# Thirteen transfers instead of sixteen for out = x + alpha·fx, with two operands sharing one buffer

## The chip, the cores and the metric

The kernel runs on one core of one Trainium2 chip, alone. The metric is the device time of the program in microseconds (us). It is a median over runs of the same program, and the profile comes from one further, profiled execution.

## The reference

```
B, S, D = 512, 32, 640          # x, fx: bfloat16, alpha: one bfloat16
def reference(x, fx, alpha):
    return x + alpha * fx
```

The arrays x and fx hold 512 · 32 · 640 values of two bytes each, 20.97 MB each, and the output is as large. So 62.9 MB cross between memory and the core's on-chip buffer whatever the kernel does, and the arithmetic is one multiply and one add for each value.

## The kernel before

Every array is seen as 128 partitions of 81,920 values. A partition's stretch is counted in columns of 512 values (K = 512), which are 1 KiB in bfloat16. There are N = 160 columns, so x alone takes 160 KiB of each partition. x has a place for the whole of itself in the buffer (`xt`), and the sum is written over it. fx has a pool `fs` of two buffers of 23 columns each (46 KiB), through which its pieces pass in turn. Together that is 206 columns.

Three lists cut the work. `X` has the six pieces in which x is loaded, `F` the seven pieces of fx, and `S` the three pieces in which the result is stored. Each piece is one transfer of all 128 partitions, so a piece of c columns is 128 rows of c KiB.

The order is written out by hand in `PLAN`, one step to a line: `x i` and `f j` load a piece, `c j` computes, `s i` stores, and `a` loads alpha and spreads it over the partitions (a matmul with a row of ones, then a copy, lines 111 to 115). All transfers are issued by SyncE (line 78), and its queue works strictly in the order of the plan: a transfer that has to wait holds up every one that stands behind it. All of `c` is VectorE's. For a piece of fx it first multiplies fx by alpha in place (line 96), then adds it onto x in place (line 99).

What makes a transfer wait in the kernel before is the pool. The third piece of fx goes into the buffer of the first, so `f 2` stands after `c 0` and waits for it, and so on for each later piece. x has no such waits, because every column of it has a place of its own. The first store is additionally held until the last piece of fx has landed (`LATE`). The last six columns of x (`x 5`) stand between that piece and the stores. The steps that the change and the prediction speak of are `load_x`, `load_f`, `compute` and `store`, with the lists above.

Of the kernel before, what the change touches and what calls it, by code (L numbers as in the profile page):

```python
# [1 line left out]

# [4 lines left out]

ACT = mybir.ActivationFunctionType
ALU = mybir.AluOpType
F32 = mybir.dt.float32  # L10
BF16 = mybir.dt.bfloat16

K = 512
P = 128


X = [(0, 8), (8, 46), (46, 92), (92, 115), (115, 154), (154, 160)]
F = [(0, 23), (23, 46), (46, 69), (69, 92), (92, 115), (115, 138), (138, 160)]
S = [(0, 64), (64, 128), (128, 160)]
N = 160  # L20

PLAN = """
x 0
x 1
a
f 0
f 1
x 2
c 0
f 2  # L30
c 1
f 3
x 3
c 2
f 4
x 4
c 3
f 5
c 4
f 6  # L40
x 5
c 5
c 6
s 0
s 1
s 2
"""
LATE = {("s", 0): ("f", 6)}


@with_exitstack
def kernel(
    ctx: ExitStack,
    tc: tile.TileContext,
    x: bass.AP,
    fx: bass.AP,
    alpha: bass.AP,
    out: bass.AP,
):
    nc = tc.nc  # L60
    xv = x.flatten_outer_dims().rearrange("(p n) d -> p (n d)", p=P)
    fxv = fx.flatten_outer_dims().rearrange("(p n) d -> p (n d)", p=P)
    ov = out.flatten_outer_dims().rearrange("(p n) d -> p (n d)", p=P)
    assert xv.shape[1] == N * K

    consts = ctx.enter_context(tc.tile_pool(name="consts", bufs=1))
    psum = ctx.enter_context(tc.tile_pool(name="psum", bufs=1, space=bass.MemoryType.PSUM))
    whole = ctx.enter_context(tc.tile_pool(name="whole", bufs=1))
    fs = ctx.enter_context(tc.tile_pool(name="fs", bufs=2))
    ctx.enter_context(tc.manual_schedule())  # L70

    sync = mybir.DependencyInfo(mybir.DependencyClass.Sync, mybir.DependencyReason.DATA)
    xt = whole.tile([P, N * K], x.dtype, name="x_t")
    ft, moved = {}, {}
    done = []

    def transfer(what, out, in_):
        r = nc.sync.dma_start(out=out, in_=in_)  # L78
        if what in LATE:
            tc.add_manual_dep(r.ins, moved[LATE[what]].ins.name, sync, reason="issue late")  # L80
        moved[what] = r
        done.append(r)

    def load_x(i):
        a, b = X[i]
        transfer(("x", i), xt[:, a * K : b * K], xv[:, a * K : b * K])

    def load_f(j):
        a, b = F[j]
        ft[j] = fs.tile([P, max(e - s for s, e in F) * K], fx.dtype, tag="f", name="f_t")  # L90
        transfer(("f", j), ft[j][:, : (b - a) * K], fxv[:, a * K : b * K])

    def compute(j):
        a, b = F[j]
        term, total = ft[j][:, : (b - a) * K], xt[:, a * K : b * K]
        nc.vector.tensor_scalar(  # L96
            out=term, in0=term, scalar1=lanes["a_f"][:], scalar2=None, op0=ALU.mult
        )
        done.append(nc.vector.tensor_tensor(out=total, in0=total, in1=term, op=ALU.add))  # L99

    def store(i):
        a, b = S[i]
        transfer(("s", i), ov[:, a * K : b * K], xt[:, a * K : b * K])

    lanes = {}

    def alpha_to_lanes():
        a_1 = consts.tile([1, 1], alpha.dtype, name="a_1")
        transfer("a", a_1[:], alpha[None, :])
        ones = consts.tile([1, P], alpha.dtype, name="ones")  # L110
        nc.vector.memset(ones[:], 1.0)  # L111
        a_ps = psum.tile([P, 1], F32, name="a_ps")
        done.append(nc.tensor.matmul(a_ps[:], ones[:], a_1[:], start=True, stop=True))  # L113
        lanes["a_f"] = consts.tile([P, 1], F32, name="a_f")
        nc.vector.tensor_copy(out=lanes["a_f"][:], in_=a_ps[:])  # L115

    does = {"x": load_x, "f": load_f, "c": compute, "s": store, "a": alpha_to_lanes}
    for step in PLAN.split("\n"):
        if step:
            what, *of = step.split()  # L120
            does[what](*map(int, of))

    rest = nc.sync.nop(nofuse=True)
    for i in done[:-1]:
        tc.add_manual_dep(rest.ins, i.ins.name, sync, reason="all but the last store")


# [1 line left out]
_INS = ['x', 'fx', 'alpha']  # L129
_OUTS = [((512, 32, 640), 'bfloat16')]  # L130


# [23 lines left out]
```

## Time and profile before

| what | value |
|---|---|
| median of 3 runs | 151.09 us (151.03 to 151.19) |
| the profiled execution | 151.26 us |
| its span, first to last instruction | 149.5 us |
| VectorE busy | 66.7 us, 45% of the span |
| DMA queue's packets, share of the 16 engines' span | 98.2% |
| bytes read and written | 41.94 MB and 20.97 MB, mean 421 GB/s |

The span is the part that the profile resolves; 1.8 us of the profiled execution lie around it. "Landing" of a transfer is the moment at which its completion is signalled. A group's line gives the number of instructions, their busy time in us and the mean of one in ns. The windows count a packet where it starts, so a short window's rate can stand above what the engines move.

### The profile page before, as it was taken

How to read it: one execution, taken by the hardware profiler on the slowest of the kernel's cores; microseconds unless marked ns; L12 is line 12 of the kernel's file. 1: busy time of each engine (PE TensorE's matmuls, PEld its weight loads, DVE VectorE, ACT ScalarE, POOL GpSimd, SP SyncE). 2: the span in 40 equal slices, each digit the busy share in tenths (PEclk: the TensorE clock that was granted, in tenths of full speed). 3: DMA queues.
4: the chain of work that ended last, by engine and by line, in shares of the span. 5: the costliest groups of instructions: out<-in, count | busy, mean ns of one | idle time of the engine just before them, and what ended most of it. 6: DMA issues, size and time to landing. Idle time of an engine off the chain costs nothing.

```text
span 149.5 us, 93 instructions
## 1 busy us (share of the span) xinstructions
PE 0.2 (0%) x1; PEld 0.1 (0%) x1; DVE 66.7 (45%) x16; POOL 0.2 (0%) x4
## 2 busy tenths in 40 slices
PE   0000000000000000000000000000000000000000
PEld 0000000000000000000000000000000000000000
DVE  0000005999950099999499104999960000000000
POOL 0000000000000000000000000000000000000000
DMA  5998999999979999999998999999996969696994
GB/s 151 463 500 354 448 410 466 435 403 466 542 303 410 466 435 403 429 460 422 443 502 353 417 460 390 458 515 438 403 561 281 561 281 561 281 561 281 456 456 210
DMA packets 2306, 62.92 MB, mean 421 GB/s; under 512 B 258, under 2 KB 258, under 8 KB 386
## 3 DMA queue, kind: packets, MB, share of 16 engines
q1 hardware_dynamic: 2306, 62.92, 98.2%
HBM read 41.94 MB, written 20.97 MB: 421 GB/s over the span
## 4 chain that ended last, share of the span: by engine, by line
DMA 41%; DVE 31%; issue 1%; SPq 1%; DVEq 0%
DMA f_t<-in_fx_dram 41%; DVE x_t L99 20%; DVE f_t L96 11%; SPq L78 1%; DVEq L96 0%
## 5 line engine op out<-in xcount | busy, mean ns | idle before, releaser
L99 DVE TENSOR_TENSOR x_t<-x_t,f_t 128x11776 bf16<-128x11776 bf16 (+1 forms) x7 | 43.8, 6254 | 0.2
L96 DVE TENSOR_SCALAR f_t<-f_t,a_f 128x11776 bf16<-128x11776 bf16 (+1 forms) x7 | 22.9, 3265 | 26.7 <-DMA f_t<-in_fx_dram 26.7
L115 DVE COPY a_f<-a_ps 128x1 f32<-128x1 f32 x1 | 0.2, 159 | 16.2 <-PE a_ps L113 16.2
L111 DVE MEMSET ones<- 1x128 bf16 x1 | 0.2, 165 | 0.8 <-PEq L140 0.8
L113 PE MATMUL a_ps<-a,ones 1*128 1x1 bf16 x1 | 0.2, 158 | 17.0 <-DMA a<-in_alpha_dram 17.0
L140 POOL MEMSET const-bfloat16-1.0<- 128x1 bf16 x1 | 0.1, 101 | 0.0
L140 POOL MEMSET const-uint8-127<- 128x1 uint8 x1 | 0.1, 101 | 0.0
L113 PEld LDWEIGHTS <-ones 1*128 1x128 bf16 x1 | 0.1, 98 | 1.0 <-DVE ones L111 1.0
L140 POOL MEMSET const-float32-0.0<- 128x1 f32 x1 | 0.1, 98 | 0.2 <-issue 0.2
L140 POOL MEMSET const-float32-1.0<- 128x1 f32 x1 | 0.1, 98 | 0.0
## 6 DMA issues: line engine op xcount, KB each, us to landing
f_t<-in_fx_dram SPq DMA_DIRECT2D x6, 2944.0 KB, 19.4
x_t<-in_x_dram SPq DMA_DIRECT2D x1, 5888.0 KB, 41.9
x_t<-in_x_dram SPq DMA_DIRECT2D x1, 4992.0 KB
x_t<-in_x_dram SPq DMA_DIRECT2D x1, 4864.0 KB, 15.9
out_dram<-x_t SPq DMA_DIRECT2D x1, 4096.0 KB, 38.1
x_t<-in_x_dram SPq DMA_DIRECT2D x1, 2944.0 KB, 22.3
f_t<-in_fx_dram SPq DMA_DIRECT2D x1, 2816.0 KB, 15.9
x_t<-in_x_dram SPq DMA_DIRECT2D x1, 1024.0 KB, 4.8
```

Source lines behind the costliest of these rows:

```text
L78: r = nc.sync.dma_start(out=out, in_=in_)
L96: nc.vector.tensor_scalar(out=term, in0=term, scalar1=lanes["a_f"][:], scalar2=None, op0=ALU.mult)
L99: done.append(nc.vector.tensor_tensor(out=total, in0=total, in1=term, op=ALU.add))
L111: nc.vector.memset(ones[:], 1.0)
L113: done.append(nc.tensor.matmul(a_ps[:], ones[:], a_1[:], start=True, stop=True))
L115: nc.vector.tensor_copy(out=lanes["a_f"][:], in_=a_ps[:])
L140: nc = _bacc.Bacc("TRN2", target_bir_lowering=False, num_devices=1)
```

## The change

The pool is gone. One tile `buf` of 206 columns holds both arrays: columns 0 to 160 are x's places, and columns 160 to 206 lie behind them. `HOME` gives the place at which each piece of fx lands. The first two pieces of fx, 34 columns each, land at 92 and 126, in the places of x's columns 92 to 160, which are loaded only when those pieces have been used. The third piece, 46 columns, lands at 160, and the last two land in its place once its halves have been used. x is loaded in five pieces and begins with one of 64 columns, where it began with one of 8. fx is loaded in five pieces. The computing steps are now a list `C` of their own, seven as before but of other sizes, because one piece of fx can serve two of them. The stores are unchanged, and so is the hold on the first of them, which is now on piece 4 of fx, its last.

```
-X = [(0, 8), (8, 46), (46, 92), (92, 115), (115, 154), (154, 160)]
-F = [(0, 23), (23, 46), (46, 69), (69, 92), (92, 115), (115, 138), (138, 160)]
+X = [(0, 64), (64, 92), (92, 114), (114, 154), (154, 160)]
+F = [(0, 34), (34, 68), (68, 114), (114, 138), (138, 160)]
+HOME = [92, 126, 160, 160, 184]
+C = [(0, 34), (34, 64), (64, 68), (68, 92), (92, 114), (114, 138), (138, 160)]
 S = [(0, 64), (64, 128), (128, 160)]
+ALL = 206
 PLAN, before:  x0 x1 a f0 f1 x2 c0 f2 c1 f3 x3 c2 f4 x4 c3 f5 c4 f6 x5 c5 c6 s0 s1 s2
 PLAN, after:   x0 a f0 f1 x1 f2 c0 x2 c1 c2 x3 c3 f3 c4 f4 x4 c5 c6 s0 s1 s2
-LATE = {("s", 0): ("f", 6)}
+LATE = {("s", 0): ("f", 4)}
...
-    fs = ctx.enter_context(tc.tile_pool(name="fs", bufs=2))
-    xt = whole.tile([P, N * K], x.dtype, name="x_t")
+    buf = whole.tile([P, ALL * K], x.dtype, name="buf")
...
     def load_f(j):
-        a, b = F[j]
-        ft[j] = fs.tile([P, max(e - s for s, e in F) * K], fx.dtype, tag="f", name="f_t")
-        transfer(("f", j), ft[j][:, : (b - a) * K], fxv[:, a * K : b * K])
+        (a, b), h = F[j], HOME[j]
+        transfer(("f", j), buf[:, h * K : (h + b - a) * K], fxv[:, a * K : b * K])

-    def compute(j):
-        a, b = F[j]
-        term, total = ft[j][:, : (b - a) * K], xt[:, a * K : b * K]
+    def compute(i):
+        a, b = C[i]
+        j = next(j for j, (s, e) in enumerate(F) if s <= a and b <= e)
+        h = HOME[j] + a - F[j][0]
+        term, total = buf[:, h * K : (h + b - a) * K], buf[:, a * K : b * K]
```

The two plans are written here in a line each; in the file a step has a line of its own.

More of the change, by code (lines that the diff above doesn't have):

```diff
@@ L14 @@
 P = 128
-X = [(0, 8), (8, 46), (46, 92), (92, 115), (115, 154), (154, 160)]
-F = [(0, 23), (23, 46), (46, 69), (69, 92), (92, 115), (115, 138), (138, 160)]
+X = [(0, 64), (64, 92), (92, 114), (114, 154), (154, 160)]
+F = [(0, 34), (34, 68), (68, 114), (114, 138), (138, 160)]
+HOME = [92, 126, 160, 160, 184]
+C = [(0, 34), (34, 64), (64, 68), (68, 92), (92, 114), (114, 138), (138, 160)]
 S = [(0, 64), (64, 128), (128, 160)]
 N = 160
+ALL = 206
 PLAN = """
 x 0
-x 1
 a
@@ L27 @@
 f 1
-x 2
-c 0
-f 2
-c 1
-f 3
-x 3
-c 2
-f 4
-x 4
[L37 to L41, printed above, removed]
+x 1
+f 2
+c 0
+x 2
+c 1
+c 2
+x 3
+c 3
+f 3
+c 4
+f 4
+x 4
 c 5
@@ L68 @@
     whole = ctx.enter_context(tc.tile_pool(name="whole", bufs=1))
-    fs = ctx.enter_context(tc.tile_pool(name="fs", bufs=2))
     ctx.enter_context(tc.manual_schedule())
     sync = mybir.DependencyInfo(mybir.DependencyClass.Sync, mybir.DependencyReason.DATA)
-    xt = whole.tile([P, N * K], x.dtype, name="x_t")
-    ft, moved = {}, {}
+    buf = whole.tile([P, ALL * K], x.dtype, name="buf")
+    moved = {}
     done = []
@@ L85, in load_x @@
         a, b = X[i]
-        transfer(("x", i), xt[:, a * K : b * K], xv[:, a * K : b * K])
+        transfer(("x", i), buf[:, a * K : b * K], xv[:, a * K : b * K])
     def load_f(j):
-        a, b = F[j]
-        ft[j] = fs.tile([P, max(e - s for s, e in F) * K], fx.dtype, tag="f", name="f_t")
-        transfer(("f", j), ft[j][:, : (b - a) * K], fxv[:, a * K : b * K])
-    def compute(j):
-        a, b = F[j]
-        term, total = ft[j][:, : (b - a) * K], xt[:, a * K : b * K]
+        (a, b), h = F[j], HOME[j]
[5 more added lines that the diff above has]
+        term, total = buf[:, h * K : (h + b - a) * K], buf[:, a * K : b * K]
         nc.vector.tensor_scalar(
@@ L102, in store @@
         a, b = S[i]
-        transfer(("s", i), ov[:, a * K : b * K], xt[:, a * K : b * K])
+        transfer(("s", i), ov[:, a * K : b * K], buf[:, a * K : b * K])
     lanes = {}
```

## The prediction

> **What bounds the kernel now.** I read the page first, for who is busy.
>
> ```profile
> span 149.5 us, 93 instructions
> PE 0.2 (0%) x1; PEld 0.1 (0%) x1; DVE 66.7 (45%) x16; POOL 0.2 (0%) x4
> ...
> DMA packets 2306, 62.92 MB, mean 421 GB/s; under 512 B 258, under 2 KB 258, under 8 KB 386
> ...
> q1 hardware_dynamic: 2306, 62.92, 98.2%
> ```
>
> The DMA engines work for 98.2% of the span. VectorE works for 45%, so it matters only if a transfer waits for it. The packets tell how a transfer is cut: 16 large transfers of 128 rows are 2048, 16 tiny ones at the end of each are 256, and alpha adds 2, which makes 2306. So a row is one packet, the 64 KiB rows of the first two stores included, and each of the 16 engines carries 8 rows of every transfer.
>
> Second, the chain of waits in order of time, for exact landings.
>
> ```profile
> 2.01 22.08 DMA f_t<-in_fx_dram
> ...
> 33.83 18.19 DMA f_t<-in_fx_dram
> ...
> 71.21 20.67 DMA f_t<-in_fx_dram
> ```
>
> Start plus duration are the landings of f0 (24.09), f2 (52.02) and f5 (91.88). Two strings of transfers lie between them: f1, x2, f2 with 92 columns in 27.93 us, and f3, x3, f4, x4, f5 with 131 columns in 39.86 us. What the queue's own waits add is the price of a column in a long row:
>
> ```profile
> SPq L123 <- DMA out_dram<-x_t: 27.9, 2, 19.3
> ```
>
> The longest wait, 19.3 us, is from the landing of s0 to that of s1, which is 64 columns: 0.3016 us a column. At that price 92 columns are 27.75 us and 131 are 39.51. The strings took 0.18 us more in 3 transfers and 0.35 us more in 5, which is 0.06 and 0.07 for each transfer. Reading the 19.3 as 19.25 or 19.35 moves this to 0.04 or 0.085. That is what a transfer costs beyond its bytes when it stands queued behind another.
>
> Third, VectorE's groups with shapes apart, for the waits that the change adds.
>
> ```profile
> L99 DVE TENSOR_TENSOR x_t<-x_t,f_t 128x11776 bf16<-128x11776 bf16 x6 | 37.8, 6292 | 0.2
> L96 DVE TENSOR_SCALAR f_t<-f_t,a_f 128x11776 bf16<-128x11776 bf16 x6 | 19.7, 3284 | 26.7 <-DMA f_t<-in_fx_dram 26.7
> ```
>
> 23 columns cost 6.29 + 3.28 us, so a column costs 0.416 us, and VectorE sat waiting for fx for 26.7 us.
>
> Fourth, the start, where x's first rows change from 8 to 64 KiB: the issues in the first microsecond, and windows.
>
> ```profile
> x_t<-in_x_dram SPq DMA_DIRECT2D x1, 1024.0 KB, 4.8
> ```
>
> ```profile
> 0.70:1.70 1.00, 0.00 (x0) 0.10 (x1) 0.17 (x1) 0.00 (x0) 1.00 0.00 0
> 1.70:2.30 0.60, 0.00 (x0) 0.00 (x0) 0.00 (x0) 0.00 (x0) 1.00 1.44 218
> 2.30:2.90 0.60, 0.00 (x0) 0.00 (x0) 0.00 (x0) 0.00 (x0) 1.00 0.54 177
> ...
> 100.45:119.79 19.34, 0.00 (x0) 0.00 (x0) 10.15 (x3) 0.00 (x0) 1.00 1.00 434
> ```
>
> The last two columns are the DMA share and GB/s. No packet starts before 1.70, although x0 is issued at 0.73. From 1.70 to 2.90 the rate is 218 and 177 GB/s, against 434 in the stretch of the first store: 237 KB where 521 KB could have gone, about 0.65 us lost. x0 lands 4.8 us after its issue, at 5.5.
>
> **The change part by part.** The bytes stay at 480 columns (320 loaded, 160 stored), or 144.8 us at 0.3016, and nothing can be saved there. Against the profiled execution (151.26 us: a span of 149.5 and 1.8 around it; the median of the runs, 151.09, lies 0.17 lower) the change moves four things.
>
> *Three transfers fewer.* Six x pieces become five and seven fx pieces five. 3 · 0.06 = 0.18 us less, 0.12 to 0.26 by the readings above. All of it is on the path, since the engines are never idle. The issues on SyncE (0.3 to 0.6 us each) lie beside running transfers before and after, so they save nothing; without that cover each would cost its third of a microsecond.
>
> The Trainium skill prices this differently: SBUF — State Buffer, section "The DMA setup-cost knee", gives every transfer a roughly fixed 2 us; three fewer would be 6 us less. The strings above do not agree: a queued transfer costs 0.06 us there, and the measurement decides.
>
> *The new waits.* I walk the new queue with 0.3016 us a column and 0.06 a transfer, from x0's landing at 5.5 + 56 · 0.3016 = 22.4. Landings: f0 32.7, f1 43.1, x1 51.6, f2 65.5, x2 72.2, x3 84.3, f3 91.6, f4 98.3, x4 100.2, s0 119.5, s1 138.9, s2 148.6. VectorE at 0.416 a column: c0 (34 columns) from 32.7 to 46.9, c1 to 59.4, c2 to 61.0, c3 from f2's landing to 75.5, c4 to 84.7, c5 from f3's landing to 101.6, c6 to 110.8.
>
> Each waiting transfer holds all that stand behind it in SyncE's queue, so what counts is whether it is released before its predecessor ends:
> - x2 waits for c0: released at 46.9, its turn at 65.5.
> - x3 waits for c0, c1 and c2: 61.0 against 72.2.
> - f3 waits for c3: 75.5 against 84.3.
> - f4 waits for c4: 84.7 against 91.6; x4 and the stores stand behind it.
>
> The narrowest margin is 6.9 us. About 1 us of a margin goes from issue to first packet (0.73 to 1.70 at the start). So the waits cost nothing, and DVE would have to be 6 us late before they did. s0 waits for the last fx landing as before, and the same six columns of x (1.9 us) still cover its start. s1 and s2 are released by c5 and c6 at 101.6 and 110.8, long before 119.5 and 138.9. Alpha landed at 17.0 behind x1; now it stands behind x0's share and lands near 22, and c0 needs it only at 32.7.
>
> *VectorE.* Seven steps before and after over the same 160 columns: nothing, with the DMA as cover.
>
> *The first rows.* What the slow stretch of the start becomes with 64 KiB rows is shown by no row here. Bounds: at best it vanishes, 0.65 us less. At worst every engine stays at the early rate for its whole first row: 1.05 MB at 198 GB/s are 5.3 us instead of 2.4 at 434, a loss of 2.9 in place of 0.65, or 2.2 us more. I take no change. The nearest row is that stretch itself: it ends by 2.9 while the engines are in their second and third 8 KiB rows, so a time after the start fits it better than a place in a row; and later transfers with rows of 23 to 64 KiB all run at the full price.
>
> [...]
>
> *Sum:* 151.26 − 0.18 = 151.08 for a profiled execution, 151.09 − 0.18 = 150.91 for the median, that is 0.12% less. A measurement of this kernel can tell about 0.2%, 0.30 us, from no change, so the saved overhead alone stays just inside.
>
> **The rivals.** *The start gets shorter* (faster). Early packets pay by the packet: with 8 KiB rows each engine starts two or three in the slow stretch, with 64 KiB one. If the first alone were slowed, between 0.12 and all of the 0.65 us would go: 150.26 to 150.79. For it: the rate of the second window (177) shows that packets started there are slow too. Against it: a slow source would make one long packet as late as three short ones.
>
> *The start gets longer* (slower). Sixteen engines that start together stay in lock step over 64 KiB. It decides from 0.48 us on (0.18 saved plus the bound of 0.30), which is a slow stretch of 0.65 + 0.48 = 1.1 us lost, and gives 151.4 to 153.1. Against it: the rows of f0 to f6 also start at one column in all partitions and show no such stretch.
>
> *A home is freed too late.* f4 after c4 has the narrowest margin. VectorE's part would have to take 6 us longer; each microsecond beyond that is one on the end. The 26.7 us of waiting speak against it.
>
> *The change doesn't do what it says.* If 64 KiB rows were loaded as two packets each, x0 would have 256 packets; at a few hundredths of a microsecond it gives back part of the 0.18, 150.95 to 151.1. The stores' count speaks against it.
>
> **How the numbers follow.** Overhead saved and start unchanged: 0.50, of which 0.42 within 0.2% and 0.08 beyond it by the small errors of the two terms. Shorter start: 0.31, all faster. Longer start: 0.12, and a late home 0.04, slower. Split rows: 0.03, within 0.2%. So faster 0.39, same 0.45, slower 0.16. The forecast is the likeliest case, 150.91, its own range 150.75 to 151.05. The range reaches into the shorter start down to 150.4, which leaves 0.05 below, and up to 151.3, which leaves about 0.15 above.
>
> **What the changed profile would show.** 13 · 144 + 2 = 1874 packets, and the landings above within 0.3 us of each other's differences. x0 should land at about 22.4: clearly earlier means the shorter start, clearly later the lock step. s2's landing minus x0's should be 126.2. SyncE's waits for VectorE grow longer but none ends after its predecessor's landing. The prediction is wrong if a stretch after 3 us shows idle DMA, or if 34 or 64 KiB rows cost other than 0.3016 us a column.

## The result and the profile after

The changed kernel takes 151.63 us (median of 7 runs, 151.46 to 151.67) where the kernel before takes 151.14 (151.03 to 151.25). The ratio is 1.003, 95% interval 1.0021 to 1.0039, so it is slower by 0.49 us. The forecast was 150.91 and its range ended at 151.3. The profiled execution took 151.63, against 151.26 before: 0.37 more.

The page, at the rows that were shown of before:

```profile
span 149.8 us, 89 instructions
PE 0.2 (0%) x1; PEld 0.1 (0%) x1; DVE 66.6 (44%) x16; POOL 0.2 (0%) x4
DMA packets 1874, 62.92 MB, mean 420 GB/s; under 512 B 210, under 2 KB 210, under 8 KB 338
q1 hardware_dynamic: 1874, 62.92, 97.8%
```

The packets are the 1874 that 13 transfers make, so a 64 KiB row is loaded as one packet. VectorE is as busy as before, and the DMA share fell from 98.2% to 97.8%. The first loss shows in the issue of x0 at 0.73 us, with its time to landing, and then in the landings of f0 and f3 on the chain of waits (start plus duration):

```profile
buf<-in_x_dram SPq DMA_DIRECT2D x1, 22.3
```

```profile
1.52 31.80 DMA buf<-in_fx_dram
...
76.16 16.07 DMA buf<-in_fx_dram
```

x0 lands at 23.0 where 22.4 was forecast, f0 at 33.3 (32.7), f3 at 92.2 (91.6). The delay of 0.6 us is there when the first transfer lands and stays as it is: after x0 the forecast intervals hold to about a tenth.

A landing is signalled by each of the 16 DMA engines for its own rows, and the trace keeps each signal. That splits the delay. Times in us:

| landing | before: mean of the engines, last | after: mean, last |
|---|---|---|
| f0 | 23.91, 24.09 | 32.60, 33.33 |
| last piece of x | 100.26, 100.45 | 100.06, 100.79 |
| s0 | 119.59, 119.79 | 119.70, 120.17 |
| s2 | 148.55, 148.73 | 148.73, 149.10 |

In the mean of the engines f0 lands at 32.60, where the forecast had 32.7 for the last. What changed is how far the last engine is behind that mean: 0.18 us before, 0.73 after. (The expectations below speak of the spread, from the first engine's signal to the last: at f0 0.42 before, 1.04 after.) In the trace's packets of x0 the first rows of the 16 engines take 2.90 to 3.95 us, where the later rows of x0 take 2.42 (110 of 112; the other two 2.50 and 2.62); the one engine with 3.95 lost 1.53 us. Before, the slowest first row of 8 KiB took 1.18 against 0.31, a loss of 0.87.

The other engines gain nothing by being ahead. From the last piece of x to s0 the mean engine takes 19.64 us and the last one 19.38: the leading engines run dry while s0 waits for the last engine's share of f4. Followed from packet to packet, eleven engines stand idle for 0.2 to 0.7 us just before their first row of s0; before, none did for more than 0.2.

The new waits are in the timeline (start, duration, engine, instruction):

```profile
47.47 12.65 SPq L79 DMA_DIRECT2D buf<-in_x_dram  x2
...
76.16 9.45 SPq L79 DMA_DIRECT2D buf<-in_fx_dram  x2
```

Each line covers two issues. x2 is issued at 47.5, x3 at 59.8, f3 at 76.2 and f4 at 85.3; their turns come at 66.1, 72.8, 84.9 and 92.2. All four are early by at least 6.9 us.

### The profile page after: what moved, and what is told of

Read it like the earlier page. It is cut to its first block, busy times and chain, and to the rows that moved or that the text cites. A ratio compares the mean times of both kernels' runs of the same rounds, so it can differ in the third digit from the quotient of the medians.

```text
span 149.8 us, 89 instructions
## 1 busy us (share of the span) xinstructions
PE 0.2 (0%) x1; PEld 0.1 (0%) x1; DVE 66.6 (44%) x16; POOL 0.2 (0%) x4
## 2 busy tenths in 40 slices
DMA packets 1874, 62.92 MB, mean 420 GB/s; under 512 B 210, under 2 KB 210, under 8 KB 338
## 3 DMA queue, kind: packets, MB, share of 16 engines
q1 hardware_dynamic: 1874, 62.92, 97.8%
## 4 chain that ended last, share of the span: by engine, by line
DVE 32%; DMA 32%; issue 6%; another core or an unknown queue 3%; SPq 0%; DVEq 0%
DMA buf<-in_fx_dram 32%; DVE buf L101 19%; DVE buf L98 13%; SPq L79 0%; DVEq L98 0%
## 5 line engine op out<-in xcount | busy, mean ns | idle before, releaser
L101 DVE TENSOR_TENSOR buf<-buf 128x12288 bf16<-128x12288 bf16 (+4 forms) x7 | 43.8, 6254 | 0.2
L98 DVE TENSOR_SCALAR buf<-buf,a_f 128x12288 bf16<-128x12288 bf16 (+4 forms) x7 | 22.9, 3264 | 22.2 <-DMA buf<-in_fx_dram 22.2
```

Source lines behind the costliest of these rows:

```text
L98: nc.vector.tensor_scalar(out=term, in0=term, scalar1=lanes["a_f"][:], scalar2=None, op0=ALU.mult)
```

## The experiments

**Short rows first again.** The changed kernel with x's first piece cut in two, everything else as it is. In this and in the cuts below, the second part is loaded right behind the first, as a step of its own in the plan, and the later pieces of x move up by one number:

```
-X = [(0, 64), (64, 92), ...
+X = [(0, 8), (8, 64), (64, 92), ...
```

> Theory 'uneven start': the slow first microsecond costs the 16 engines the same in the mean (0.65 us) whatever the rows, but with 64 KiB rows one engine is held far more than the rest and carries that to the end. With 8 KiB rows first, the last engine is again only 0.2 us behind the mean, and two transfers fewer than before are left: 151.0 us, 0.12 below before and 0.6 below the changed kernel; every load lands within 0.4 us over its engines. Rival 'homes': the shared places, the new waits or the other piece sizes cost the time: 151.7, as the changed kernel plus one transfer.

Measured: 151.04 us (150.88 to 151.17), ratio to before 0.9992 (0.9983 to 1.0001). The chain shows f0's landing:

```profile
2.01 30.71 DMA buf<-in_fx_dram
```

That is 32.72 instead of 33.33, and the last engine is 0.26 us behind the mean; the mean itself, 32.46, is 0.14 earlier. The whole loss of the changed kernel goes with one cut at its start; homes, waits and sizes are cleared.

**Long rows first in the kernel before.** The same step in the other kernel, with nothing else of the change:

```
-X = [(0, 8), (8, 46), (46, 92), ...
+X = [(0, 46), (46, 92), ...
```

> The kernel before, with x's first two pieces (8 and 38 columns) as one of 46: one transfer fewer, nothing else. 'Uneven start': the spread of the landings over the engines grows from 0.4 to near 1 us and the time to 151.3 to 151.5. 'Homes': one transfer fewer, 151.08, spread 0.4.

Measured: 151.59 us, ratio 1.0027 (1.0018 to 1.0036). f0 lands at 24.39, where it landed at 24.09:

```profile
1.52 22.87 DMA f_t<-in_fx_dram
```

The last engine is 0.51 us behind the mean at f0, where it was 0.18. One transfer fewer and 46 KiB rows first make the old kernel as slow as the new one.

**The cut put late.** As many transfers as with the cut at 8, but long rows first:

```
-X = [(0, 64), (64, 92), ...
+X = [(0, 56), (56, 64), (64, 92), ...
```

> The changed kernel with x's first piece cut at column 56: as many transfers as with the cut at 8, but the long rows come first. 'Uneven start': the spread stays near 1 us and the time is 151.7, the changed kernel plus 0.06. If the number or the length of the transfers were at work, it would go the way of the cut at column 8.

Measured: 151.62 us (1.0026, 1.0017 to 1.0035), f0's last engine 0.40 behind the mean. It isn't the number of transfers.

**How short, and how much.** Four more cuts of the same piece, at columns 1, 4, 16 and 32 beside the 8 above:

```
-X = [(0, 64), (64, 92), ...
+X = [(0, 1), (1, 64), (64, 92), ...
+X = [(0, 4), (4, 64), (64, 92), ...
+X = [(0, 16), (16, 64), (64, 92), ...
+X = [(0, 32), (32, 64), (64, 92), ...
```

> The changed kernel with x's first piece cut at column 1: 8 packets of 1 KiB for each engine, then rows of 63 KiB. If the slow stretch is a stretch of time (to 2.9 us) in which a long row is shared out unevenly, these packets are through before it ends, the long rows begin inside it and the spread is near 1 us again: 151.6. If only the first packets of an engine pay, whatever their size, the spread is small and the time 151.0 or a little less. 'Homes': 151.7.

> The changed kernel with x's first piece cut at column 4: rows of 4 KiB, 0.16 us each at the full rate, eight of them 1.3 us. If the first piece only has to outlast the slow stretch (about 1.1 us) in rows shorter than it, this does as well as the cut at 8: spread 0.5 us, 151.05. If the stretch is also a matter of bytes, so that a piece of 512 KB is too small to absorb it, the rows of 60 KiB behind it catch it as they did behind one column: spread 0.8 us or more, 151.4 to 151.9.

> The changed kernel with x's first piece cut at column 16: 16 KiB rows first. The uneven start should lie between the cut at 8 (spread 0.5 us, 151.04) and none (1.07, 151.63): spread 0.6 to 0.8 and 151.1 to 151.4, if the spread grows with the first rows; near 0.5 and 151.05 if rows only have to be shorter than the slow stretch.

> The changed kernel with x's first piece cut at column 32: 32 KiB rows first, which take 1.21 us at the full rate and so outlast the slow stretch (about 1.1 us), as rows of 16 KiB (0.61 us) don't. 'Uneven start' with the row's length against the stretch: an engine can be held in its one row for the whole stretch, spread 0.7 to 1 us, 151.3 to 151.6. If only far longer rows do it, spread 0.5 and 151.1.

| x's first rows | time, us | ratio to before, 95% interval | profiled execution, us | its f0 lands (last engine behind the mean), us |
|---|---|---|---|---|
| 1 KiB | 151.91 | 1.0045 (1.0033 to 1.0058) | 152.14 | 33.84 (0.91) |
| 4 KiB | 151.04 | 0.9991 (0.9982 to 1.0) | 151.32 | 33.02 (0.52) |
| 8 KiB | 151.04 | 0.9992 (0.9983 to 1.0001) | 151.03 | 32.72 (0.26) |
| 16 KiB | 151.08 | 0.9994 (0.9984 to 1.0003) | 151.11 | 32.86 (0.27) |
| 32 KiB | 151.45 | 1.0015 (1.0006 to 1.0024) | 151.21 | 32.91 (0.31) |
| 56 KiB | 151.62 | 1.0026 (1.0017 to 1.0035) | 151.48 | 33.16 (0.40) |
| 64 KiB (no cut) | 151.63 | 1.003 (1.0021 to 1.0039) | 151.63 | 33.33 (0.73) |

The last two columns are of one execution, and there the time follows f0's last landing: it is 118.25 to 118.32 us more in all seven, and in the four kernels below with a `hold` or another row pitch. From the mean landing the difference runs from 118.5 to 119.2, so it is the last engine that sets the end. The mean moves too, from 32.46 with 8 KiB rows to 32.93 with 1 KiB, and the last engine's place behind it is only a part of the loss. The profiled executions of 4 and 32 KiB were the slowest and the second fastest of their kernels; for the choice of a row length the time column decides.

Both ends are dear. With 1 KiB rows the eight packets of an engine run at full rate (most in 0.044 to 0.06 us) and are through within 0.8 us; the 63 KiB rows behind them then take up to 3.70 us instead of 2.38, and single engines get their first one only at 3.3 and 4.1 us. A reading that fits all seven is that the first piece has to outlast the slow stretch, and in rows that are shorter than it: 4 to 16 KiB do both (8 rows of 4 KiB are 1.3 us, one row of 16 KiB is 0.6), 32 KiB rows of 1.2 us are on the edge. The expectation for 4 KiB that counted bytes fails by the time.

**What makes the start slow.** Three kernels take one thing each away from the changed kernel. Where one has a `hold`, it is a step `h` of the plan, placed ahead of the transfer that waits for it.

All issues behind x0 held until VectorE has filled unused columns:

```
+    def hold():
+        moved["h"] = nc.vector.memset(buf[:, 160 * K : 206 * K], 0.0)
-LATE = {("s", 0): ("f", 4)}
+LATE = {"a": "h", ("s", 0): ("f", 4)}
```

> The changed kernel, with alpha's transfer and all issues behind it held until VectorE has filled an unused part of the buffer (about 6 us), so that x's 64 KiB rows start with nothing being issued beside them. Theory 'issues disturb': the slow stretch comes from the issues of the next transfers between 1.1 and 3.5 us; then the first packets take the usual 2.42 us, x0 lands at 22.0 instead of 23.0 and the time falls to 150.6. Theory 'lock step' (sixteen engines start together on rows 160 KiB apart): the stretch stays, first packets of 2.9 to 4 us, 151.6. Theory 'first use' (the path from memory is slow for about a microsecond when first used): as lock step.

```profile
0.72 0.38 SPq L83 DMA_DIRECT2D buf<-in_x_dram  x1
3.25 9.87 DVE L80 MEMSET buf<- 128x11776 uint32 x1 [3.25 <-issue]
...
13.15 0.29 SPq L83 DMA_DIRECT2D a<-in_alpha_dram  x1
```

The timeline shows x0 alone until 13.15, and still its first rows take 2.47 to 3.70 us and the time is 151.60 (1.0033, 1.0022 to 1.0044). Issues do not disturb.

The first 114 columns laid out as one contiguous part of the arrays and the rest as another, so that rows lie 114 or 46 KiB apart instead of 160; stores of 64, 50 and 46 columns:

```
+        low = flat[: P * CUT * K].rearrange("(p k) -> p k", p=P)
+        high = flat[P * CUT * K :].rearrange("(p k) -> p k", p=P)
```

> The changed kernel with another place of the rows in memory: the first 114 columns of the buffer hold one contiguous part of the arrays, the rest the other, so that the rows of a transfer lie 114 or 46 KiB apart instead of 160. The stores are 64, 50 and 46 columns, the transfers as many as before. 'Lock step': the first packets are no longer slowed or much less, x0 lands near 22.2 and the time is 150.7 to 151.0. 'First use' and 'issues disturb': no change, 151.6, first packets of 2.9 to 4 us.

Measured: 151.50 us (1.0025, 1.0015 to 1.0034), first rows of 2.44 to 3.66 us. If the pitch has a share, it is 0.1 us; a lock step by pitch is not what these runs show at 160 and 114 KiB. The Trainium skill (DMA: Bandwidth & Descriptors, "Latency and other measured facts") gives 207 GB/s at a row pitch of 512 KiB beside 214 that it calls full, and clear losses at 2 MiB and more, from which it infers such a lock step; no run here has a pitch like these.

The whole queue started later, x0 too:

```
+        moved["h"] = nc.vector.memset(buf[:, 160 * K : 180 * K], 0.0)
-LATE = {("s", 0): ("f", 4)}
+LATE = {("x", 0): "h", ("s", 0): ("f", 4)}
```

> The changed kernel, with its first transfer held until VectorE has filled 20 unused columns (about 2.7 us), all else after it. 'Program's start' (something at the start of the program disturbs until about 3 us): the first packets, now after 4.4 us, take the usual 2.42 us, and x0 lands 1.4 us later than its issue would give without disturbance, at about 24.2 to 24.5. 'Lock step', 'first use' and 'issues disturb': the stretch moves with the first packets, which take 2.9 to 4 us again; x0 lands at 25 to 26 and the time is 154 to 154.5.

```profile
1.87 4.33 DVE L80 MEMSET buf<- 128x5120 uint32 x1 [1.87 <-issue]
...
6.22 0.38 SPq L83 DMA_DIRECT2D buf<-in_x_dram  x1
```

The fill took 4.33 us instead of 2.7 and began at 1.87, so x0 was issued at 6.22. Its first rows, from 7.23, took 2.92 to 3.73 us, and the time is 157.26: 5.63 more, with the start 5.49 later. The stretch moves with the first packets; the program's start has no part in it.

**Is it only the first use?** The changed kernel with f0 held until x0 has landed and VectorE has copied six columns, so that the engines run dry once more:

```
+        moved["h"] = nc.vector.tensor_copy(out=buf[:, 200 * K : 206 * K], in_=buf[:, : 6 * K])
-LATE = {("s", 0): ("f", 4)}
+LATE = {("f", 0): "h", ("s", 0): ("f", 4)}
```

> The changed kernel, with fx's first piece held until x's first has landed and VectorE has copied six of its columns, so that the DMA engines fall idle for some 3 us and start anew with 34 KiB rows. If any start after idleness is slow, f0's first packets take 1.6 to 2.2 us instead of 1.29 and its landings spread by 0.8 us or more anew. If only the program's first use is slow, they take 1.29 us and the landings of f0 lie within 0.3 us, as all engines start together. Time about 154.5 in both.

```profile
22.90:24.80 1.90, 0.00 (x0) 0.00 (x0) 0.94 (x1) 0.00 (x0) 1.00 0.00 0
```

```profile
buf<-in_fx_dram SPq DMA_DIRECT2D x1, 4352.0 KB, 13.2
```

The window's last columns are the DMA share and GB/s: no packet starts for 1.9 us. The last row of x0 ends at 22.52, and f0's first starts at 24.83. f0, issued at 23.87, lands 13.2 later, at 37.07. Its first rows of 34 KiB take 1.63 to 2.25 us, against 1.29 for a usual one, and the last engine lands 0.70 behind the mean. Time 155.37 in one run, 3.74 above the changed kernel, more than the 2.9 expected. So this start from idle is slow in mid-program too, not only at first use.

**One transfer fewer elsewhere.** Short rows first, x's last two pieces in one, and the first store no longer held:

```
-X = [(0, 8), (8, 64), (64, 92), (92, 114), (114, 154), (154, 160)]
-LATE = {("s", 0): ("f", 4)}
+X = [(0, 8), (8, 64), (64, 92), (92, 114), (114, 160)]
+LATE = {}
```

> The changed kernel with 8 KiB rows first, x's last two pieces as one of 46 columns, and the first store no longer held: 13 transfers again, without the late start. At 0.06 us a transfer it is 150.98, 0.06 below the cut at column 8 and 0.16 below before. If stores queued behind loads without the hold disturb them, the stretch around the change from loads to stores grows and it is above 151.1.

Measured: 151.61 us (1.0027, 1.0018 to 1.0036), 0.57 above the kernel with the hold. The start is as good as any (f0's last engine 0.21 behind the mean). The loss is where loads meet stores:

```profile
93.40:97.00 3.60, 0.00 (x0) 0.00 (x0) 3.57 (x2) 0.00 (x0) 1.00 1.08 463
97.00:99.70 2.70, 0.00 (x0) 0.00 (x0) 2.70 (x1) 0.00 (x0) 1.00 0.89 284
```

The rate falls to 284 GB/s in the last 2.7 us before the first row of a store starts (the windows count a row where it starts; over both it is 386, against 434 at the full price): in the packets, 27 of the last 32 rows loaded (two for each engine) take 1.0 to 1.44 us instead of 0.84, with stores queued right behind them. The hold on s0 and the six columns of x that cover it are worth 0.6 us together; which of the two would do alone wasn't run.

## Why the prediction was wrong

- **Three transfers fewer, 0.18 us: right, as far as the runs can tell.** From the last landing of x0 to that of s2 the forecast was 126.2 us; it took 149.10 − 23.03 = 126.07. At the last piece of x, the engines are in the mean 0.20 us ahead of before (100.06 against 100.26). With the start mended by one more transfer, two fewer than before gain 0.10 us where 0.12 was reckoned, though the interval just takes in no change. That is far from the 2 us a transfer of the Trainium skill (SBUF — State Buffer, "The DMA setup-cost knee"), as the prediction held.
- **The new waits, nothing: right.** The margins are 18.6, 13.0, 8.7 and 6.9 us against 18.6, 11.2, 8.8 and 6.9 forecast. x3 has more because it waits for c1 and not for c2: it ends at column 154, and the last piece of fx that c2 reads lies at 156. (By the prediction's own prices f1 and x1 come at 43.0 and 51.5, where it wrote 43.1 and 51.6; nothing hangs on it.)
- **VectorE, nothing, and one packet a row: right.** 66.6 us busy, 1874 packets.
- **The first rows, "I take no change": this step failed.** The mean loss did not change, as argued, and f0's mean landing of 32.60 is the forecast's 32.7. But the end is set by the last of 16 engines, and the prediction reckoned with one rate for all. Measured at the last engine, the term is 23.03 − 22.4 = 0.6 us. Then −0.18 + 0.6 = +0.4 us, against 0.37 in the profiled execution. The same one rate stands behind "the same six columns of x (1.9 us) still cover its start" for s0. They cover it for the last engine; the leading ones are through with them up to 0.7 us before their first row of s0 starts, and lose their lead there.
- **The rival "the start gets longer" had the place, the sign and the point from which it decides** (0.48 us; it was 0.6), and 151.63 lies in its 151.4 to 153.1. Its mechanism was not the one: no lock step through whole rows, for the first rows lost 0.74 us in the mean, where whole rows at the early rate would have lost 2.9. It was one slow microsecond that fell unevenly on the engines. Its chance of 0.12 was too low. That the rows of f0 to f6 show no such stretch was a poor argument against it, since those transfers were queued behind running ones; started from idle, f0 shows it too.

What stays open is why the slow stretch holds one engine so much longer than the rest when rows are long, and what in the chip makes a start from idle slow. The runs exclude the issues beside it and the start of the program, and leave the row pitch at most a small share.

## What to carry to other kernels

When a kernel keeps all DMA engines busy, the end belongs to the last engine, and an engine that falls behind stays behind as long as every transfer gives all engines the same rows (here 0.73 to 0.75 us behind the mean from f0 to the last load): look at the spread of the landings, not at the mean rate. Open a queue that starts from idle with a piece that outlasts the slow start in short rows (here 4 to 16 KiB, eight to an engine), and only then send long rows. Merging queued transfers is worth 0.06 us apiece here, so it pays only where it leaves that opening, and the changeover from loads to stores, alone.

## What the runs showed of the hardware that was not expected

- Each start from idle that was run has a slow stretch of about a microsecond, also, in the one run that tried it, in the middle of the program: first rows of 34 KiB took up to 2.25 us instead of 1.29 after 1.9 us in which no packet started.
- Packets of 1 KiB hardly pay it themselves (most took 0.044 to 0.06 us at the start, the slowest 0.32), but the long rows behind them do (up to 3.70 instead of 2.38).
- Loads with stores queued right behind them were slow in the one kernel without the hold: rows of 0.84 us took up to 1.44.
